# First group's values projected alone, VectorE exponentials from the first unit on, and the last output tile split over three engines

## The chip, the cores and the metric

The kernel runs on one core of a Trainium2 chip. The metric is the device time of one execution in microseconds (us). The engines are TensorE (PE, matrix products into PSUM), VectorE (DVE), ScalarE (ACT), GpSimd (POOL) and SyncE (SP, which issues most of the DMAs). A weight load of TensorE is shown as PEld.

## The reference

x is a 2048 x 512 bf16 matrix. Two branches are computed from it and mixed row by row with a gate:

```python
def _A_ref(x, wqkv, wo):            # 32 heads of 16
    qkv = (x @ wqkv).reshape(B, S, 3, H, Dh).transpose(2, 0, 3, 1, 4)
    q, k, v = qkv[0], qkv[1], qkv[2]
    scores = jnp.einsum("bhqd,bhkd->bhqk", q, k) * (Dh ** -0.5)
    p = softmax(scores, axis=-1)
    o = jnp.einsum("bhqk,bhkd->bhqd", p, v)
    return o.transpose(0, 2, 1, 3).reshape(B, S, D) @ wo

def _B_ref(x, w_gate, w_up, w_down):  # hidden size 1792
    return (silu(x @ w_gate) * (x @ w_up)) @ w_down

g = sigmoid((x * gate_w).sum(-1, keepdims=True))
out = g * _A_ref(x) + (1 - g) * _B_ref(x)
```

The attention has 32 x 2048 x 2048 exponentials. In the kernel they are 2048 banks of 128 keys x 512 queries.

## The kernel before

Heads are handled in eight groups of four, queries in four blocks of 512, keys in 16 tiles of 128. A unit is one group of heads for one block of queries; there are 32 units, in the order of `UNIT` (L114): group 0 for all four query blocks first, then the other groups block by block. Within a unit a slot is one key tile, with four banks, one for each head, so there are 512 slots and 64 banks to a unit. Group 0's keys and queries have a path of their own at the start: they are projected with zero-padded weights and need no DMA to reach the rows where the scores want them.

A bank is a product of keys and queries (`score`, L608) into PSUM. Then one of two engines takes the exponential. ScalarE takes banks in pairs (`emit_pair`, L621): one activation of 128x1024, tile s_t to tile e_t. VectorE takes them in blocks of four, one bank of each head of the group (`emit_d`, L641): for each bank one step from d_t to y_t, and for the four together six steps of 128x2048 on y_t, z_t and u_t, the last of which writes y_t. Afterwards `pv` (L720) multiplies by the values (vaug: for every head a column of ones and 16 columns of values; 32 columns are read, so those of the next head stand in the product too, in rows that nobody uses). A block whose unit has been closed by then gets its product in a bank of its own (x_ps) and an addition on VectorE.

The order of the instructions on TensorE, ScalarE and VectorE is written out at build time by a planner. It keeps a planned clock for each of the three engines (`Plan`), with a cost for each step, and emits what fits. Work that is not attention comes in chains of pieces (`Chain`, `Pacer`, L17 to L73), each with a slot of release and a due slot: projections of keys, queries and values, the gate, the two FFN products, the down product and the output product. `side` (L1069) gives out a piece only if the pacer has credit, which grows by slot with the most pressing due work. `begin` (L1059) forces chains that a slot needs. `force` emits all of a chain, and pays the VectorE steps owed to it. VectorE's steps are owed at emission and paid by `fill_dve` (L695): first the step of a waiting d_t, then owed evictions, then block steps. `to_vector` (L1086) says whether the next bank goes to VectorE: none in unit 0, no new block behind bank 50 of a unit (behind bank 4 in the last), none while three blocks are live or more than 6 us of block steps wait.

At the start SP issues the four transposing loads of x (L174), then the values' weights wv (512 columns, into the tile rb, L184) and the rest of wqk; ScalarE's queue issues the first 64 columns of the query and key weights (L178). GpSimd and VectorE set constants; lo_t, far_t and bsel (L245 to L248) are three small VectorE steps whose result the key bounds of later groups use (`k_bound`, L376). TensorE then projects group 0's keys and the first queries; VectorE reduces the keys' largest absolute values (kpart), makes kneg from them, TensorE multiplies that with the queries' absolute values (bp), and VectorE adds the bound to the queries (qx). In between stands `v_now` (L873), which projects four value tiles over all 512 columns, evicted by ScalarE. The other 12 value tiles are chains (`v_pieces`, L381) with due slot tt + 3, evicted by VectorE into vaug.

FFN chains are due between `f0` = 44 and `f1` = 504 (L944). They use the tile mt for the hidden activations.

After the last unit closes there is a tail: the output product for the last two groups in two parts (`last_mm`, L1168), reciprocals of the softmax sums, their product with the last unit's output (on_l), and `store` (L818) for each of the four output tiles: one VectorE step from PSUM, gate and an accumulated part (acc, which lies in kaug's memory), and one DMA issued by SP. All VectorE steps there follow each other in the written order.

Of the kernel before, what the change touches and what calls it, by code (L numbers as in the profile page):

```python
# [78 lines left out]
def kernel(  # L79
# [100 lines left out]

    rb = big.tile([P, NB, QBW], BF16, name="rb")
    wv = rb[:, :, :]

    nc.sync.dma_start(out=wv, in_=A_wqkv[:, 2 * D:3 * D].rearrange("(dc p) c -> p dc c", p=P))  # L184
    for c0 in (D, 0):
        nc.sync.dma_start(out=wqk[:, :, c0 + 64:c0 + D],
                          in_=A_wqkv[:, c0 + 64:c0 + D].rearrange("(dc p) c -> p dc c", p=P))
# [39 lines left out]
    for g in range(1, G):  # L227

        nc.vector.memset(kaug[:, g, :].bitcast(F32), 1.0019378662109375)
    vaug = big.tile([P, KT, G * 4 * VC + 16], BF16, name="vaug")  # L230
    nc.gpsimd.memset(vaug[:, :, G * 4 * VC:], 0.0)
    nc.gpsimd.memset(
        vaug[:, :, 0:G * 4 * VC].rearrange("p t (h c) -> p t h c", c=VC)[:, :, :, 0:1], 1.0)

# [5 lines left out]
    for h in range(8):  # L240
        c = 2 * (h % 4) + h // 4
        nc.gpsimd.memset(lo_t[:, c:c + 1], float(DH * h))
    far_t = const.tile([P, 8], F32, name="far_t")

    nc.vector.tensor_scalar(out=lo_t[:], in0=lo_t[:], scalar1=pidx[:, 0:1], scalar2=None, op0=ALU.subtract)  # L245
    nc.vector.tensor_scalar(out=far_t[:], in0=lo_t[:], scalar1=-float(DH) + 0.5, scalar2=-1.0,
                            op0=ALU.is_gt, op1=ALU.mult)
    nc.vector.scalar_tensor_tensor(out=bsel[:, :], in0=lo_t[:], scalar=0.5, in1=far_t[:],  # L248
                                   op0=ALU.is_lt, op1=ALU.mult)
# [131 lines left out]
    def v_pieces(tt, act_evac=False):  # L381
        st = {}

        def pc(h):
            def f():
                if h == 0:
                    st["p"] = m_tile("vp")
                for dc in (2 * h, 2 * h + 1):
                    mm(st["p"][:, 0:D], lhsT=xT[:, dc, tt * P:(tt + 1) * P], rhs=wv[:, dc, :],
                       start=(dc == 0), stop=(dc == DC - 1))  # L390
                spend("F", 2)
                if h == 1 and act_evac:
                    end()
                elif h == 1:
                    later(0.75, end)
            return f

        def end():
            dst = vaug[:, tt, 0:G * 4 * VC].rearrange("p (h c) -> p h c", c=VC)[:, :, 1:1 + DH]
            sv = st["p"][:, 0:D].rearrange("p (h c) -> p h c", c=DH)  # L400
            if act_evac:
                act(out=dst, in_=sv, func=ACT.Copy)
            else:
                vec.tensor_copy(out=dst, in_=sv)
            m_free(plan.pe if act_evac else plan.dve)
        return [(2, pc(0), True), (2, pc(1), False)]


# [311 lines left out]
    def pv(bs, last):  # L720


        un = bs[0] // (4 * KT)
        extra = un < closed
        if extra:
            o = m_tile("x_ps")
        else:
            if un not in o_of:
                while un and un - 1 not in osbs:
                    pay()  # L730
                plan.pe = max(plan.pe, o_end[0])
                o_of[un] = ps_o.tile([P, QBW], F32, tag="o", name="o_ps")
            o = o_of[un]
        for b in bs:
            n, j = b // 4, HEADS[b % 4]
            first = extra or (un, j) not in begun
            begun.add((un, j))
            c0 = (4 * UNIT[un][1] + j) * VC
            if n < KT and n in v_chain:
                force(v_chain[n])  # L740
            mm(o[32 * j:32 * j + 32, :], lhsT=vaug[:, n % KT, c0:c0 + 32], rhs=e_of.pop(b),
               start=first, stop=extra or last, tile_position=(0, 32 * j), skip_group_check=True)
            e_left.pop(b, None)
        spend("C", 1, max(e_end.pop(b, 0.0) for b in bs))
        if extra:
            def add():
                blocks[un] -= 1
                vec.tensor_tensor(out=(of_of if blocks[un] else osbs)[un][:, :], in0=of_of[un][:, :], in1=o[:, :],
                                  op=ALU.add)
                m_free(plan.dve)  # L750
                if not blocks[un]:
                    finish(un)
            later(0.6, add)
# [119 lines left out]
    def v_now(tt):  # L873
        for _, f, _ in v_pieces(tt, act_evac=True):
            f()

    act(out=q0r[:, :], in_=qp0[:, :], func=ACT.Copy)
    for i in range(2):
        vec.tensor_reduce(out=kpart0[:, i:i + 1], in_=kp0[i][:, :], axis=AX.X, op=ALU.max,
                          apply_absolute_value=True)  # L880
        vec.tensor_copy(out=ones_h[i][:], in_=onescol[:])
        v_now(i)
        act(out=kaug[:, 0, i * 2 * QBW:(i + 1) * 2 * QBW], in_=kp0[i][:, :], func=ACT.Identity,
            bias=ones_h[i][:, 0:1], scale=1.0)
        if i == 0:
            vec.tensor_scalar(out=kneg1, in0=bsel0, scalar1=kpart0[:, 0:1], scalar2=None, op0=ALU.mult)
            vec.tensor_scalar(out=aq0[:, :].bitcast(U16), in0=q0r[:, :].bitcast(U16), scalar1=0x7FFF, scalar2=None,
                              op0=ALU.bitwise_and)
    vec.scalar_tensor_tensor(out=kneg0, in0=bsel0, scalar=kpart0[:, 1:2], in1=kneg1,
                             op0=ALU.mult, op1=ALU.min)  # L890
    v_now(2)
# [7 lines left out]
    V0 = 4  # L899
    v_now(3)  # L900
    plan.dve = plan.act = plan.pe


    pace = Pacer()
    need = {}
    v_chain = {}
    for tt in range(V0, KT):
        v_chain[tt] = pace.add(v_pieces(tt), 0, tt + 3)
    prev = []
    for qb in range(1, QB):  # L910
        d = qb * KT
# [29 lines left out]
    order_ = [(qb, fc) for qb in range(QB) for fc in range(FC)]  # L941
    prev = []
    fin_prev = []
    f0, f1 = 44, SLOTS - 8  # L944
    per = (f1 - f0) / QB
    for qb in range(QB):
        a0 = f0 + per * qb
# [65 lines left out]
    def pv_ready(now):  # L1013

        if late and (now is None or late[0][0] <= now):
            un = late[0][1][0] // (4 * KT)
            if un == closed or un < closed and (now is None or m_ready() is not None and m_ready() <= now):
                return late[0][1]
        if done < SLOTS and done // KT == closed and not (now is not None and done in v_chain
                                                          and not v_chain[done].done()):  # L1020
            bs = [b for b in range(4 * done, 4 * done + 4) if b not in vset]
            if all(b in e_of for b in bs) and (now is None or max(e_end[b] for b in bs) <= now):
                if closed in o_of or now is None or (not closed or closed - 1 in osbs) and o_end[0] <= now:
                    return bs
        return None

    def pvs_ready(now):

        k = n = 0
        for ready, bs in late[:2]:  # L1030
            un = bs[0] // (4 * KT)
            if ready <= now and (un == closed or un < closed and k == 0 and m_ready() is not None and m_ready() <= now):
                k += 1
        for n in (done, done + 1):
            if n < SLOTS and n // KT == closed and not (n in v_chain and not v_chain[n].done()):
# [50 lines left out]
    def to_vector():  # L1086

        un, at_ = divmod(nxt, 4 * KT)
        if vcur:
            if nxt % 4 in [b % 4 for b in vcur["b"]]:  # L1090
                return 0
            return 2 if at_ >= 4 * KT - 4 * (NV - vcur["i"]) else 1
        if not un or at_ > (50 if un < UNITS - 1 else 4) or y_live[0] >= 3 or sum(v[0] for v in vops) > 6:
            return 0
        return 1

    while nxt < nb:
# [4 lines left out]
        if pairs[0] - min(e_left.values(), default=pairs[0]) >= EB - 1:  # L1102

            for m in (done, done + 1):
                while m in v_chain and not v_chain[m].out():
                    emit_piece(v_chain[m])
            next_pv()
            continue
        room = s_end[pairs[0] % 2] - plan.pe
# [110 lines left out]
```

## Time and profile before

| | |
|---|---|
| Median of 4 runs | 875.71 us (874.95 to 876.65) |
| Profiled execution, time | 874.95 us |
| Profiled execution, span | 873.2 us |
| First exponential starts / last one ends | 19.85 / 863.8 us |
| ScalarE busy | 845.4 us (97%) |
| TensorE busy | 799.7 us (92%) |
| VectorE busy | 786.9 us (90%) |
| GpSimd busy | 7.1 us |
| ScalarE exponentials (two banks each) | 882 |
| VectorE blocks (four banks each) | 71 |

A profile line of a group reads: line of the kernel (that of a helper, where one is used: L158 for matmuls, L161 for ScalarE, L167 for VectorE's ordered steps), engine, operation, output tile, input tiles, shapes and count; then busy time in all, mean ns of one; then the engine's idle time just before them, and what ended it. Instructions of an engine overlap a little, so starts are closer together than durations say. A matmul's duration includes its way through the array; consecutive ones start more closely than that.

### The profile page before, as it was taken

The page shows a single profiled execution, that of the slowest core. Times are in us where ns is not written, and L with a number is a line of the kernel's source. Part 1 is how long each engine was busy: PE and PEld are TensorE (multiplying, and loading weights), DVE is VectorE, ACT ScalarE, POOL GpSimd, SP SyncE. Part 2 cuts the span into 40 slices and gives each one's busy share as a digit, 9 for nine tenths or more (in the row PEclk, how much of TensorE's full clock was granted, in tenths as well). Part 3 has the DMA queues.
Part 4 walks back from the last instruction along what each step waited for, and adds up shares of the span by engine and source line. Part 5 has one row for each costly group of instructions (what it writes and reads, how often), then busy time and mean ns, then how long its engine had stood idle before and what let it go on. Part 6 is the DMA issues. An engine that isn't in the chain of part 4 may idle for free.

```text
span 873.2 us, 14286 instructions
## 1 busy us (share of the span) xinstructions
PE 799.7 (92%) x5168; PEld 207.8 (24%) x5168; DVE 786.9 (90%) x1103; ACT 845.4 (97%) x947; POOL 7.1 (1%) x29
## 2 busy tenths in 40 slices
PE   5999999999999899999989899899998989989986
PEld 2222222222222222222222222222222222222221
DVE  6379999999999999999999999999999998999984
ACT  3999999999999999999999999999999999999995
POOL 3000000000000000000000000000000000000000
PEclk9999999999999999999999999999999999999998
DMA  8301121131101112210011121110011121000000
GB/s 213 106 1 28 29 50 34 24 67 31 31 12 26 40 33 72 53 37 11 4 30 33 34 55 45 42 28 4 4 25 35 36 57 49 21 10 4 5 20 24
DMA packets 87535, 31.98 MB, mean 37 GB/s; under 512 B 75120, under 2 KB 87016, under 8 KB 87464
## 3 DMA queue, kind: packets, MB, share of 16 engines
q1 hardware_dynamic: 86408, 30.94, 14.4%
q8 instruction: 40, 0.66, 0.3%
q10 hardware_dynamic: 1056, 0.13, 0.1%
q14 instruction: 31, 0.25, 0.1%
HBM read 20.83 MB, written 2.34 MB: 27 GB/s over the span
## 4 chain that ended last, share of the span: by engine, by line
ACT 43%; PE 36%; issue 10%; DVE 9%; SPq 1%; DMA 1%; DVEq 0%; ACTq 0%
ACT e_t L161 39%; PE s_t L158 13%; PE o_ps L158 7%; DVE y_t L167 4%; PE d_t L158 4%; PE dps L158 4%; ACT th L161 3%; PE gp L158 3%; DVE u_t L167 2%; PE up L158 1%; PE qp L158 1%; SPq L174 1%; PE kp L158 1%; PE vp L158 1%; PE a_ps L158 1%
## 5 line engine op out<-in xcount | busy, mean ns | idle before, releaser
L161 ACT ACTIVATE e_t<-s_t 128x1024 bf16<-128x1024 f32 x882 | 821.9, 1079 | 4.4 <-PE s_t L158 3.1
L158 PE MATMUL s_t<-qx,kaug 64*128 64x512 bf16 x1656 | 330.2, 385 | 50.0 <-ACT e_t L161 48.1
L167 DVE TENSOR_SCALAR y_t<-d_t 128x512 uint16<-128x512 f32 x284 | 195.1, 687 | 29.7 <-PE d_t L158 26.3
L158 PEld LDWEIGHTS <-kaug 64*128 64x128 bf16 x2048 | 100.0, 93 | 379.0 <-issue 375.9
L158 PE MATMUL o_ps<-e_t,vaug 128*32 128x512 bf16 x1764 | 173.5, 388 | 0.4 <-ACT e_t L161 0.3
L158 PE MATMUL d_t<-qx,kaug 64*128 64x512 bf16 x264 | 99.6, 377 | 0.3 <-DVE y_t L167 0.3
L167 DVE TENSOR_TENSOR y_t<-y_t,u_t 128x2048 uint16<-128x2048 uint16 x71 | 86.6, 1219 | 0.9
L167 DVE TENSOR_TENSOR u_t<-u_t 128x2048 f16<-128x2048 f16 x71 | 86.5, 1218 | 0.8
L167 DVE TENSOR_TENSOR u_t<-u_t,z_t 128x2048 f16<-128x2048 f16 x71 | 86.4, 1217 | 0.4
L158 PEld LDWEIGHTS <-vaug 128*32 128x32 bf16 x2048 | 45.5, 94 | 133.3 <-issue 129.4
L158 PE MATMUL dps<-wd_t,mt 128*128 128x512 bf16 x224 | 67.8, 384 | 0.0
L158 PE MATMUL gp<-xT,wg 128*128 128x512 bf16 x224 | 67.8, 384 | 0.0
L158 PE MATMUL up<-xT,wu 128*128 128x512 bf16 x224 | 65.7, 384 | 0.0
L167 DVE TENSOR_SCALAR y_t<-y_t 128x2048 uint16<-128x2048 uint16 x71 | 48.9, 688 | 1.2
L167 DVE TENSOR_SCALAR u_t<-z_t 128x2048 f16<-128x2048 uint16 x71 | 48.7, 686 | 0.7
L167 DVE TENSOR_SCALAR z_t<-y_t 128x2048 uint16<-128x2048 uint16 x71 | 48.6, 684 | 0.1
L167 DVE SCALAR_TENSOR_TENSOR gs<-th,gp 128x512 bf16<-128x512 bf16 x56 | 38.2, 681 | 4.2 <-ACT th L161 3.7
L167 DVE SCALAR_TENSOR_TENSOR mt<-gs,up 128x512 bf16<-128x512 bf16 x56 | 38.2, 682 | 2.2
L161 ACT ACTIVATE th<-gp 128x512 bf16<-128x512 f32 x56 | 36.4, 650 | 0.0
L158 PEld LDWEIGHTS <-mt 128*128 128x128 bf16 x263 | 16.1, 99 | 42.9 <-issue 36.1
L158 PE MATMUL s_t<-on,kaug 64*128 64x512 bf16 x108 | 21.7, 383 | 3.1 <-ACT e_t L161 2.7
L158 PEld LDWEIGHTS <-wu 128*128 128x128 bf16 x224 | 13.7, 97 | 32.0 <-issue 27.6
(101 smaller groups left out, 352.8 us busy)
## 6 DMA issues: line engine op xcount, KB each, us to landing
wg<-in_B_w_gate_dram SPq DMA_DIRECT2D x56, 128.0 KB
wu<-in_B_w_up_dram SPq DMA_DIRECT2D x56, 128.0 KB
on<-osb SPq DMA_DIRECT2D x120, 16.0 KB
rb<-rr SPq DMA_DIRECT2D x15, 128.0 KB
wd_t<-in_B_w_down_dram SPq DMA_DIRECT2D x1, 1792.0 KB
qx<-qst SPq DMA_DIRECT2D x112, 16.0 KB
out_dram<-o_t SPq DMA_DIRECT2D x12, 128.0 KB
kaug<-on SPq DMA_DIRECT2D x20, 64.0 KB
```

Source lines behind the costliest of these rows:

```text
L158: ordered(nc.tensor.matmul(*args, **kw))
L161: ordered(nc.scalar.activation(*args, **kw))
L167: return lambda *a, **kw: ordered(f(*a, **kw))
L174: nc.sync.dma_start_transpose(out=xT[:, dc, :], in_=x[:, dc * P:(dc + 1) * P])
```

## The change

It has six parts.

1. Values' weights come in two loads: the first 64 columns (group 0) on ScalarE's queue, behind the first query and key weights; the other 448 on SP as before.
2. Group 0's values are projected alone, four key tiles into one bank (`v0_pieces`): the first four tiles before the first unit, in one place between the two reductions, evicted by one ScalarE step; the other three chains with due slots 5, 9 and 13. The other groups' values (`v_pieces`, now 448 columns) are 16 chains released at slot 2, due at slots 12 + 3 tt, and forced by the first product that needs them (unit 4, slot 64). `v_of` and `v_done` tell which chain a slot needs.
3. The steps for lo_t, far_t and bsel move behind the first queries' update, and kneg1 behind both reductions. GpSimd sets 16 more columns of vaug to zero.
4. `to_vector` allows VectorE's banks from bank 8 of unit 0 on, and in the last unit new blocks up to bank 24 (before: 4).
5. FFN chains start being due at slot 72 instead of 44, and `side` gives out a piece without credit if a chain needed within 12 slots is not out.
6. In the tail, tile 0 of the last output is scaled by ScalarE from PSUM into an f32 tile and added by GpSimd; VectorE stores tiles 1 to 3; tile 0's DMA is issued by SP behind theirs.

```diff
     wv = rb[:, :, :]
-    nc.sync.dma_start(out=wv, in_=A_wqkv[:, 2 * D:3 * D].rearrange("(dc p) c -> p dc c", p=P))
+    nc.scalar.dma_start(out=wv[:, :, 0:64], in_=A_wqkv[:, 2 * D:2 * D + 64].rearrange("(dc p) c -> p dc c", p=P))
+    nc.sync.dma_start(out=wv[:, :, 64:D], in_=A_wqkv[:, 2 * D + 64:3 * D].rearrange("(dc p) c -> p dc c", p=P))
...
+    nc.gpsimd.memset(vaug[:, :, 4 * VC:4 * VC + 16], 0.0)
...
-    nc.vector.tensor_scalar(out=lo_t[:], in0=lo_t[:], scalar1=pidx[:, 0:1], scalar2=None, op0=ALU.subtract)
...
+    def v0_pieces(t0, act_evac=False):
+        st = {}
+        def pc(i):
+            def f():
+                if i == 0:
+                    st["p"] = m_tile("vp")
+                for dc in range(DC):
+                    mm(st["p"][:, 64 * i:64 * i + 64], lhsT=xT[:, dc, (t0 + i) * P:(t0 + i + 1) * P],
+                       rhs=wv[:, dc, 0:64], start=(dc == 0), stop=(dc == DC - 1))
+                spend("F", V0_MM)
+                if i == 3 and act_evac:
+                    end()
+                elif i == 3:
+                    later(0.35, end)
+            return f
+        def end():
+            dst = vaug[:, t0:t0 + 4, 0:4 * VC].rearrange("p t (h c) -> p t h c", c=VC)[:, :, :, 1:1 + DH]
+            sv = st["p"][:, 0:256].rearrange("p (t h c) -> p t h c", h=4, c=DH)
+            if act_evac:
+                act(out=dst, in_=sv, func=ACT.Copy)
+            else:
+                vec.tensor_copy(out=dst, in_=sv)
+            m_free(plan.pe if act_evac else plan.dve)
+        return [(V0_MM, pc(i), i == 0) for i in range(4)]
+    V0_MM = 1.8
+    def v_pieces(tt):
...
-                    mm(st["p"][:, 0:D], lhsT=xT[:, dc, tt * P:(tt + 1) * P], rhs=wv[:, dc, :],
+                    mm(st["p"][:, 64:D], lhsT=xT[:, dc, tt * P:(tt + 1) * P], rhs=wv[:, dc, 64:D],
                        start=(dc == 0), stop=(dc == DC - 1))
...
-        v_now(i)
         act(out=kaug[:, 0, i * 2 * QBW:(i + 1) * 2 * QBW], in_=kp0[i][:, :], func=ACT.Identity,
             bias=ones_h[i][:, 0:1], scale=1.0)
         if i == 0:
-            vec.tensor_scalar(out=kneg1, in0=bsel0, scalar1=kpart0[:, 0:1], scalar2=None, op0=ALU.mult)
             vec.tensor_scalar(out=aq0[:, :].bitcast(U16), in0=q0r[:, :].bitcast(U16), scalar1=0x7FFF, scalar2=None,
                               op0=ALU.bitwise_and)
+        if i == 0:
+            for _, f, _ in v0_pieces(0, act_evac=True):
+                f()
+    vec.tensor_scalar(out=kneg1, in0=bsel0, scalar1=kpart0[:, 0:1], scalar2=None, op0=ALU.mult)
...
-    for tt in range(V0, KT):
-        v_chain[tt] = pace.add(v_pieces(tt), 0, tt + 3)
+    for i in range(1, KT // 4):
+        v_chain[i] = pace.add(v0_pieces(4 * i), 0, 4 * i + 1)
+    v_rest = [pace.add(v_pieces(tt), 2, int(12 + 3 * tt)) for tt in range(KT)]
+    def v_of(n):
+        if n < KT:
+            return v_chain.get(n // 4)
+        return v_rest[n - QB * KT] if QB * KT <= n < QB * KT + KT else None
...
-    f0, f1 = 44, SLOTS - 8
+    f0, f1 = 72, SLOTS - 8
...
-        c = pace.next(plan.slot) if pace.credit > 0 else None
+        due = any(not c.out() for n in range(plan.slot, plan.slot + 12) for c in need.get(n, []))
+        c = pace.next(plan.slot) if pace.credit > 0 or due else None
...
-        if not un or at_ > (50 if un < UNITS - 1 else 4) or y_live[0] >= 3 or sum(v[0] for v in vops) > 6:
+        if nxt < 8 or at_ > (50 if un < UNITS - 1 else 24) or y_live[0] >= 3 or sum(v[0] for v in vops) > 6:
             return 0
...
-    for tq in range(TQ):
-        store(qb * TQ + tq, a_ps[tq], acc[0][:, tq, :], mt[:, tq, :])
+    t0 = qb * TQ
+    scaled = work.tile([P, QBW], F32, tag="of", name="scaled", bufs=1)
+    act(out=scaled[:, :], in_=a_ps[0][:, 0:D], func=ACT.Identity, scale=gval[:, t0:t0 + 1])
+    nc.gpsimd.tensor_tensor(out=mt[:, 0, :], in0=scaled[:, :], in1=acc[0][:, 0, :], op=ALU.add)
+    for tq in range(1, TQ):
+        store(t0 + tq, a_ps[tq], acc[0][:, tq, :], mt[:, tq, :])
+    nc.sync.dma_start(out=out_f[t0 * P:(t0 + 1) * P, :], in_=mt[:, 0, :])
```

More of the change, by code (lines that the diff above doesn't have):

```diff
@@ L243 @@
     far_t = const.tile([P, 8], F32, name="far_t")
-    nc.vector.tensor_scalar(out=lo_t[:], in0=lo_t[:], scalar1=pidx[:, 0:1], scalar2=None, op0=ALU.subtract)
[L246 to L249, printed above, removed]
     nc.gpsimd.memset(wo_l[:], 0.0)
@@ L379, in k_bound @@
                           scalar2=None, op0=ALU.mult)
-    def v_pieces(tt, act_evac=False):
+    def v0_pieces(t0, act_evac=False):
[24 more added lines that the diff above has]
+    def v_pieces(tt):
         st = {}
@@ L388, in f @@
                 for dc in (2 * h, 2 * h + 1):
-                    mm(st["p"][:, 0:D], lhsT=xT[:, dc, tt * P:(tt + 1) * P], rhs=wv[:, dc, :],
+                    mm(st["p"][:, 64:D], lhsT=xT[:, dc, tt * P:(tt + 1) * P], rhs=wv[:, dc, 64:D],
                        start=(dc == 0), stop=(dc == DC - 1))
                 spend("F", 2)
[L392 to L395, printed above, removed]
+                if h == 1:
+                    later(0.7, end)
             return f
         def end():
[L399 to L405, printed above, removed]
+            dst = vaug[:, tt, 4 * VC:G * 4 * VC].rearrange("p (h c) -> p h c", c=VC)[:, :, 1:1 + DH]
+            vec.tensor_copy(out=dst, in_=st["p"][:, 64:D].rearrange("p (h c) -> p h c", c=DH))
+            m_free(plan.dve)
         return [(2, pc(0), True), (2, pc(1), False)]
@@ L738, in pv @@
             c0 = (4 * UNIT[un][1] + j) * VC
-            if n < KT and n in v_chain:
-                force(v_chain[n])
+            if v_of(n) is not None:
+                force(v_of(n))
             mm(o[32 * j:32 * j + 32, :], lhsT=vaug[:, n % KT, c0:c0 + 32], rhs=e_of.pop(b),
@@ L872 @@
     kneg1 = mt[:, 3, 2 * P:3 * P]
-    def v_now(tt):
-        for _, f, _ in v_pieces(tt, act_evac=True):
-            f()
     act(out=q0r[:, :], in_=qp0[:, :], func=ACT.Copy)
@@ L885 @@
         if i == 0:
-            vec.tensor_scalar(out=kneg1, in0=bsel0, scalar1=kpart0[:, 0:1], scalar2=None, op0=ALU.mult)
             vec.tensor_scalar(out=aq0[:, :].bitcast(U16), in0=q0r[:, :].bitcast(U16), scalar1=0x7FFF, scalar2=None,
                               op0=ALU.bitwise_and)
+        if i == 0:
+            for _, f, _ in v0_pieces(0, act_evac=True):
+                f()
+    vec.tensor_scalar(out=kneg1, in0=bsel0, scalar1=kpart0[:, 0:1], scalar2=None, op0=ALU.mult)
     vec.scalar_tensor_tensor(out=kneg0, in0=bsel0, scalar=kpart0[:, 1:2], in1=kneg1,
                              op0=ALU.mult, op1=ALU.min)
-    v_now(2)
     bp0 = ps_d.tile([P, QBW], F32, tag="d", name="bp0")
@@ L898 @@
                                  in1=q0[0][:, v, :], op0=ALU.mult, op1=ALU.add)
-    V0 = 4
-    v_now(3)
+    vec.tensor_scalar(out=lo_t[:], in0=lo_t[:], scalar1=pidx[:, 0:1], scalar2=None, op0=ALU.subtract)
+    vec.tensor_scalar(out=far_t[:], in0=lo_t[:], scalar1=-float(DH) + 0.5, scalar2=-1.0,
+                            op0=ALU.is_gt, op1=ALU.mult)
+    vec.scalar_tensor_tensor(out=bsel[:, :], in0=lo_t[:], scalar=0.5, in1=far_t[:],
+                                   op0=ALU.is_lt, op1=ALU.mult)
     plan.dve = plan.act = plan.pe
@@ L906, with v_done @@
     v_chain = {}
-    for tt in range(V0, KT):
-        v_chain[tt] = pace.add(v_pieces(tt), 0, tt + 3)
+    for i in range(1, KT // 4):
[5 more added lines that the diff above has]
+        return v_rest[n - QB * KT] if QB * KT <= n < QB * KT + KT else None
+    def v_done(n):
+        return v_of(n) is None or v_of(n).done()
     prev = []
@@ L1018, in pv_ready @@
                 return late[0][1]
-        if done < SLOTS and done // KT == closed and not (now is not None and done in v_chain
-                                                          and not v_chain[done].done()):
+        if done < SLOTS and done // KT == closed and (now is None or v_done(done)):
             bs = [b for b in range(4 * done, 4 * done + 4) if b not in vset]
@@ L1034, in pvs_ready @@
         for n in (done, done + 1):
-            if n < SLOTS and n // KT == closed and not (n in v_chain and not v_chain[n].done()):
+            if n < SLOTS and n // KT == closed and v_done(n):
                 bs = [b for b in range(4 * n, 4 * n + 4) if b not in vset]
@@ L1104 @@
             for m in (done, done + 1):
-                while m in v_chain and not v_chain[m].out():
-                    emit_piece(v_chain[m])
+                while v_of(m) is not None and not v_of(m).out():
+                    emit_piece(v_of(m))
             next_pv()
```

## The prediction

> **What bounds the kernel now.** I read the page's head first, then the groups of instructions, then the chain that ended last, then busy times by stretch, and last the order of time at both ends.
>
> ```profile
> PE 799.7 (92%) x5168; PEld 207.8 (24%) x5168; DVE 786.9 (90%) x1103; ACT 845.4 (97%) x947; POOL 7.1 (1%) x29
> ...
> L161 ACT ACTIVATE e_t<-s_t 128x1024 bf16<-128x1024 f32 x882 | 821.9, 1079 | 4.4 <-PE s_t L158 3.1
> L158 PE MATMUL s_t<-qx,kaug 64*128 64x512 bf16 x1656 | 330.2, 385 | 50.0 <-ACT e_t L161 48.1
> L167 DVE TENSOR_SCALAR y_t<-d_t 128x512 uint16<-128x512 f32 x284 | 195.1, 687 | 29.7 <-PE d_t L158 26.3
> ```
>
> The reader is to see ScalarE as the bound of the body: 882 exponentials with only 4.4 us of idle before them all, while TensorE waits 48.1 us for ScalarE. TensorE and VectorE are close behind. The first exponential starts at 19.85 us and the last ends at 863.8, so the span of 873.2 is 19.85 of start, 844 of ScalarE, 9.4 of tail. In a stretch of 27 exponentials (25.04 us with one whole 1.08 at the end) the pitch is (25.04-1.08)/26 = 0.922 us for a pair of banks. A block of four banks that VectorE takes is two pairs: 1.84 us less of ScalarE.
>
> The start and its chain:
>
> ```profile
> 10.10 4.73 DMA rb<-in_A_wqkv_dram
> 14.87 1.04 PE vp L158 x4
> 15.93 0.60 ACT vaug L161
> 16.53 1.00 ACT kaug L161
> 17.53 0.49 ACT vaug L161
> 18.02 1.01 ACT kaug L161
> 19.02 0.97 ACT vaug L161 x2
> ```
>
> Columns: start, duration, what. The first exponential stands behind the whole values load (rb, 4.73 us) and four ScalarE evictions of values. Of the DMA queues in the first 20 us, the one that ScalarE issued to (packets, MB, share of the time of 16 engines):
>
> ```profile
> q10 hardware_dynamic: 1056, 0.13, 4.2%
> ```
>
> ```profile
> 20.00:48.00 28.00, 26.77 (x164) 7.08 (x162) 10.16 (x15) 28.00 (x31) 0.00 (x0) 1.00 0.35 95
> 48.00:76.00 28.00, 27.22 (x172) 6.74 (x170) 24.64 (x37) 27.37 (x31) 0.00 (x0) 1.00 0.01 4
> 836.00:864.00 28.00, 23.01 (x152) 6.09 (x149) 18.29 (x29) 27.27 (x30) 0.00 (x0) 0.90 0.01 3
> ```
>
> Columns: stretch, length, busy PE, PEld, DVE, ACT, POOL, then clock, DMA share, GB/s. VectorE works 10 of 28 us in the first unit and 18 in the last one, against 26 to 27 in the body. TensorE is full in the first unit.
>
> **The change part by part.** The sum is made against the profiled execution (span 873.2, time 874.95; the median of the runs is 875.71, 0.76 more).
>
> *Start.* Now TensorE begins the values at 14.87, when rb lands, and the bound's product bp, queued behind 12 of them, starts at 17.46 though its operand is ready at 16.28 and TensorE is free from 13.58. After: 16 products of 64 columns need only the small load. Each lies between the 4-column dt products (0.24/4 = 0.06) and the vp ones (0.215); I take 0.1, so they end at about 15.2 and bp waits only for VectorE. On VectorE far_t and bsel (0.16 each) leave the place between the two reductions and kneg1 (0.25) moves behind the second, so kneg0 still ends near 16.2. bp then starts at 16.35 instead of 17.46: 1.1 us earlier, and so do the two qx updates (1.41) and the first scores. ScalarE keeps pace: q0r to 14.2, kaug to 15.4, one smaller value eviction to 15.9, kaug to 17.0. Its bound is the 19.99 at which its last value eviction ends now.
> The small load is a third transfer on ScalarE's queue, ahead of the table load; ScalarE is idle until 13.61, so its 0.5 us of issue is free. Its packets are like those of the two wqk loads: 4.2% of 20 us is 0.84 us of all 16 engines for two, so 0.42 for one, and the engines are full (share 1.0 and more from 4 to 12 us) with the transposes that gate the last kp products at 12.34. Net -0.7; ends -1.1 (the load hides in a gap) and +0.4 (bp gains nothing). The page "DMA: Bandwidth & Descriptors" of the Trainium skill, Specifications, asks for at least 512 B per transfer and so speaks against a slice of 128 B rows; by it the load is worse than its bytes, which the row of that queue already holds.
> The moved bsel steps have their first user many slots on; the added zeroing on GpSimd is like the one of 0.31 us there, and GpSimd ends at 8.0 us with the first value eviction near 15: both nothing, at worst 0.4 of VectorE if it were already loaded.
>
> *VectorE's banks in unit 0.* From 23 us to 48 VectorE is idle about 15.7 us, and 3.4 in the next 28, where the body leaves about 1.5: 15.7 - 1.3 (5% stays idle) + 1.9 = 16.3. Against it stand the evictions: now 12 of 0.69 in the body = 8.3; after, 16 of 448 columns at 0.6 (between 0.41 and 0.69) and 3 of 256 at 0.4, 10.8 to 11.1, so 2.8 more. Left 13.5 us. A block costs VectorE (by the rows of y_t, z_t and u_t) 4 x 0.687 + 0.684 + 0.686 + 0.688 + 1.218 + 1.217 + 1.219 = 8.46, and by 32 late additions of 0.68 for 71 blocks 0.3 more: 8.8. That is 1.5 blocks, 1.5 x 1.84 = -2.8 us. The ends are 0 (the blocks come here and are missing later) and three blocks, -5.5.
>
> *TensorE.* Does it have room? At measured pitches unit 0 costs now: 32 score pairs at 0.33, 16 value products at 0.30, 24 projection pieces at 0.53, three q0 pieces at 0.53: 29.7 for 29.5 us of ScalarE, full. After, for 28 pairs (25.8 us): 9.2 + 8 single banks at 0.21 = 1.7, 4.8, twelve first-group pieces at 0.5 (four weight loads of 0.096 and a switch of 0.1) = 6.0, q0 1.6: 23.3, and 2.5 left for five of 32 rest pieces at 0.48. The other 27, 13 us, go to slots 16 to 60, out of which the FFN start (slot 44 to 72) takes 28 slots of about 0.37 us = 10.3. That work returns between slots 72 and 504, where the 48 us that TensorE waits for ScalarE can cover it. I take +0.5; ends 0 and +3.0 (a third of the 10.3 shows). The queue behind each rest eviction is VectorE's: products of the first group read 15 columns of the next group's values, so a late rest eviction holds TensorE; the evictions come in emission order with spare slots, hence nothing, inside the same upper end.
>
> *Last unit.* A second block may start up to bank 24. VectorE is free of the unit-30 work at 845.7 and then has the three on products 1.1, block one 5.4 by starts, four a_ps steps 2.6; the second block adds 4 x 0.62 + 5.4. Together 17.0, to 862.7 without a gap, 863.7 with one us of the 3.9 that it now waits for a_ps. ScalarE ends 1.84 earlier, at 862.0, against 863.8. So only about half a us is left: -0.5; ends -1.8 and +2.7 (all gaps stay: 866.6).
>
> *Tail.*
>
> ```profile
> 867.75 1.41 DVE L167 SCALAR_TENSOR_TENSOR mt<-al,gval,kaug 128x512 bf16<-128x512 f32 x2
> 868.53 2.31 SPq L823 DMA_DIRECT2D out_dram<-mt  x4
> 869.08 1.40 DVE L167 SCALAR_TENSOR_TENSOR mt<-a_l,gval,kaug 128x512 bf16<-128x512 f32 x2
> ```
>
> Four VectorE steps at 0.68 end at 870.48; the last of four stores (0.35 to issue) goes out at 870.5. After, three end at about 869.9, and store four waits for ScalarE (0.6, from 867.6) and GpSimd's add. That add has no row: between half of the 0.951 of a 128x1024 fill and the 2.27 of the strided 128x512 one; nearest is the select, which reads and writes, 0.292 for 128, so 1.17 for 512. It ends at about 869.5; the last store, behind tile 3's on SP, goes at 870.2. -0.3; ends -0.5 and +0.3. The Trainium skill, "GPSIMD Engine Reference", Performance versus the Vector engine, gives GpSimd twice VectorE's time for such an add and keeps elementwise work on VectorE; by its 4.5 us for 2048 columns the add would be 1.1 us, still hidden by three VectorE steps, an estimate that no row here shows.
>
> Sum: -0.7 - 2.8 + 0.5 - 0.5 - 0.3 = -3.8: 871.2 for the profiled execution, 872.0 for the median.
>
> **The rivals.**
> *More blocks (chance 0.18).* Three blocks in unit 0 kept to the end, and the last one's block in full: -0.7 - 5.5 - 1.8 - 0.3 = -8.3, 867.4. For it: 17 idle us. Against it: VectorE is at 26 to 27 of 28 after that, so the evictions moved later displace blocks.
> *The gain is eaten by TensorE (0.22).* One block net, and the denser TensorE makes ScalarE wait 2.5: -0.7 - 1.8 + 2.5 = 0.0, 874 to 876.5. For it: 27.22 of 28 busy in the second stretch, with the idle of 0.43 us before an exponential at 56.56. Against it: TensorE's 48 us of waiting. The same time results if the change doesn't do what it says, blocks in unit 0 being taken from later ones: -0.7, 875.
> *Slower (0.10).* A third block in the last unit. It is started if the second has its four banks by bank 24 with no more than 6 us of VectorE steps planned ahead. Then 7.9 us more stand before the end, 863.7 becomes 871.6, +7.8 on that path, with the rest -3.3 net: +4 to +5, 880. It decides from about 5 us of lateness on. Against it: VectorE is busy with reciprocals until 845.7, so those six us are still planned when the second is full.
> The forecast itself has 0.50: 869.5 to 873.9.
>
> **How the numbers follow.** A measurement here tells about 0.2% (1.75 us): 873.96 to 877.46 is the same. Faster takes the forecast 0.50 and the first rival 0.18, and a little of the second: 0.70. Same: most of the second, 0.19. Slower: the third and an end of the unknowns, 0.11. The range leaves a tenth on each side: 867.3 to 876.6. The forecast's own is 869.5 to 873.9.
>
> **What would show it.** Start: first exponential near 19.1 with no value load in the chain. Blocks: y_t steps from about 23 us, 72 to 74 final y_t steps instead of 71, fewer exponentials at the same 0.92 pitch. TensorE: idle before exponentials under 8 us in all. Last unit: final y_t step near 863. Tail: 9 us from the last exponential. Wrong would be: no fall in exponentials, or ScalarE waiting for scores in the first 100 us, or a last y_t step after 865.

## The result and the profile after

The changed kernel takes 877.45 us at the median, the kernel before 875.81 us in the runs beside it. The ratio is 1.0019, with a 95% interval from 1.0012 to 1.0026: 0.19% slower, where 0.42% faster was forecast, and outside the forecast range (867.3 to 876.6). The profiled execution has a span of 875.5 us against 873.2.

The head of the page and the groups of exponentials and of VectorE's bank steps, after:

```profile
PE 805.2 (92%) x5232; PEld 210.2 (24%) x5232; DVE 806.8 (92%) x1133; ACT 840.3 (96%) x941; POOL 8.7 (1%) x31
...
L161 ACT ACTIVATE e_t<-s_t 128x1024 bf16<-128x1024 f32 x878 | 818.1, 1092 | 5.0 <-PE s_t L158 3.8
...
L167 DVE TENSOR_SCALAR y_t<-d_t 128x512 uint16<-128x512 f32 x292 | 200.6, 687 | 33.3 <-PE d_t L158 30.1
```

VectorE has 73 blocks (292 banks) instead of 71, ScalarE four exponentials less. So VectorE did take banks off ScalarE, as forecast. The span splits as follows:

| | before | after | difference |
|---|---|---|---|
| first exponential starts | 19.85 | 20.14 | +0.3 |
| from there to the end of the last one | 843.95 | 838.97 | -5.0 |
| from there to the end of the span | 9.4 | 16.4 | +7.0 |

The body won 5.0 us, and the end lost 7.0. The end of the changed kernel in order of time (start, duration, engine, line, operation, tiles; in brackets the idle time before it, and what ended it):

```profile
863.60 0.69 DVE L167 TENSOR_SCALAR y_t<-y_t 128x2048 uint16<-128x2048 uint16 x1
864.21 0.68 DVE L167 COPY of<-o_ps 128x512 f32<-128x512 f32 x1
864.35 0.62 PE L158 MATMUL x_ps<-y_t,vaug 128*32 128x512 bf16 x4 [4.78 <-DVE y_t L167]
...
868.24 1.03 PE L158 MATMUL al<-wo_l,on_l 128*128 128x512 bf16 x2 [0.40 <-DVE on_l L167]
869.06 1.06 PE L158 MATMUL a_l<-wo_l,on_l 128*128 128x512 bf16 x2
869.31 0.69 ACT L161 ACTIVATE scaled<-al,gval 128x512 f32<-128x512 f32 x1 [10.20 <-PE al L158]
870.03 0.75 DVE L167 SCALAR_TENSOR_TENSOR mt<-al,gval,kaug 128x512 bf16<-128x512 f32 x1 [1.25 <-ACT scaled L161]
870.08 1.27 POOL L1225 TENSOR_TENSOR mt<-scaled,kaug 128x512 bf16<-128x512 f32 x1 [861.73 <-ACT scaled L161]
870.70 1.40 DVE L167 SCALAR_TENSOR_TENSOR mt<-a_l,gval,kaug 128x512 bf16<-128x512 f32 x2
871.37 0.37 SPq L1228 DMA_DIRECT2D out_dram<-mt  x1
871.84 1.38 SPq L845 DMA_DIRECT2D out_dram<-mt  x3
```

Three things are to be seen. The last exponential ended at 859.11, but TensorE stands 4.78 us until the last step of the last unit's second block. Behind that its products run at half speed: the last two into al, of 512 columns each, take 1.03 us where they took 0.60 before:

```profile
867.11 0.60 PE L158 MATMUL al<-wo_l,on_l 128*128 128x512 bf16 x2 [0.40 <-DVE on_l L167]
```

And in the stores VectorE waits for ScalarE's scaling, and SP issues tile 0's store (L1228) first, not last: the other three stand behind it until GpSimd is done at 871.35.

Three stretches of the start, of before and then of after (columns: stretch, length, busy PE, PEld, DVE, ACT, POOL with instructions, then granted clock, DMA share, GB/s):

```profile
15.00:20.00 5.00, 4.77 (x23) 1.86 (x22) 3.22 (x7) 4.07 (x7) 0.00 (x0) 1.00 0.69 217
20.00:30.00 10.00, 9.22 (x58) 2.41 (x55) 2.77 (x4) 10.00 (x12) 0.00 (x0) 1.00 0.98 265
30.00:40.00 10.00, 9.91 (x60) 2.59 (x57) 5.32 (x8) 10.00 (x12) 0.00 (x0) 1.00 0.00 1
```

```profile
15.00:20.00 5.00, 1.86 (x21) 0.91 (x19) 4.59 (x11) 2.99 (x4) 0.00 (x0) 0.85 0.89 287
20.00:30.00 10.00, 9.86 (x66) 3.12 (x65) 3.36 (x9) 8.80 (x10) 0.00 (x0) 0.56 0.93 258
30.00:40.00 10.00, 9.65 (x68) 2.73 (x68) 9.90 (x16) 10.00 (x13) 0.00 (x0) 1.00 0.05 9
```

After the change TensorE works 1.86 of the five us before the first exponential, where it worked 4.77, and in the ten us behind that its granted clock is 0.56 instead of 1.00. ScalarE, the bound, then works 8.80 of 10 us instead of 10. What TensorE does around bp, the bound's product, before and then after:

```profile
14.87 2.75 PE L158 MATMUL vp<-rb,xT 128*128 128x512 bf16 x12 [1.29 <-DMA rb<-in_A_wqkv_dram]
17.46 0.38 PE L158 MATMUL bp<-aq,mt 128*128 128x512 bf16 x1
```

```profile
15.34 0.63 PE L158 MATMUL vp<-rb,xT 128*128 128x64 bf16 x16
18.26 0.39 PE L158 MATMUL bp<-aq,mt 128*128 128x512 bf16 x1 [2.29 <-DVE mt L167]
19.49 1.36 PE L158 MATMUL s_t<-qx,kaug 64*128 64x512 bf16 x4 [0.84 <-DVE qx L167]
```

The 16 small value products are done in 0.63 us, and TensorE then stands 2.29 us ahead of bp and 0.84 us behind it.

### The profile page after: what moved, and what is told of

Its sections match the earlier page's. It is cut to its first block, busy times and chain, and to the rows that moved or that the text cites. A ratio compares the mean times of both kernels' runs of the same rounds, so it can differ in the third digit from the quotient of the medians.

```text
span 875.5 us, 14437 instructions
## 1 busy us (share of the span) xinstructions
PE 805.2 (92%) x5232; PEld 210.2 (24%) x5232; DVE 806.8 (92%) x1133; ACT 840.3 (96%) x941; POOL 8.7 (1%) x31
## 4 chain that ended last, share of the span: by engine, by line
PE 45%; ACT 37%; issue 8%; DVE 7%; DMA 1%; SPq 1%; DVEq 0%; ACTq 0%
ACT e_t L161 34%; PE s_t L158 16%; PE o_ps L158 8%; PE d_t L158 5%; PE dps L158 4%; PE gp L158 3%; DVE y_t L167 3%; ACT th L161 3%; DVE u_t L167 2%; PE up L158 2%; PE qp L158 1%; PE vp L158 1%; PE kp L158 1%; PE a_ps L158 1%; PE x_ps L158 1%
## 5 line engine op out<-in xcount | busy, mean ns | idle before, releaser
L167 DVE TENSOR_SCALAR y_t<-d_t 128x512 uint16<-128x512 f32 x292 | 200.6, 687 | 33.3 <-PE d_t L158 30.1
L158 PE MATMUL o_ps<-e_t,vaug 128*32 128x512 bf16 x1756 | 170.5, 387 | 0.0
L158 PE MATMUL d_t<-qx,kaug 64*128 64x512 bf16 x276 | 104.9, 380 | 0.3 <-DVE y_t L167 0.3
L167 DVE TENSOR_TENSOR u_t<-u_t 128x2048 f16<-128x2048 f16 x73 | 89.0, 1219 | 0.9
L167 DVE TENSOR_TENSOR y_t<-y_t,u_t 128x2048 uint16<-128x2048 uint16 x73 | 89.0, 1219 | 0.7
L167 DVE TENSOR_TENSOR u_t<-u_t,z_t 128x2048 f16<-128x2048 f16 x73 | 88.8, 1217 | 0.4
L158 PE MATMUL vp<-rb,xT 128*128 128x448 bf16 (+1 forms) x128 | 22.2, 286 | 0.0
```

Source lines behind the costliest of these rows:

```text
L158: ordered(nc.tensor.matmul(*args, **kw))
L167: return lambda *a, **kw: ordered(f(*a, **kw))
```

## The experiments

All ratios are to the kernel before in runs beside it; the changed kernel itself has 1.0019 [1.0012, 1.0026].

| kernel | median us | ratio | 95% interval |
|---|---|---|---|
| last unit's limit back at 4 (e1_last4) | 873.31 | 0.9967 | 0.9948 to 0.9985 |
| no split of the last tile (e2_nosplit) | 875.64 | 1.0003 | 0.9986 to 1.0020 |
| kernel before with limit 24 (e3_before24) | 877.79 | 1.0021 | 1.0006 to 1.0037 |
| idle products at the start (e4_warm) | 875.43 | 0.9987 | 0.9975 to 0.9999 |
| e1, e2 and e4 together (e5_combined) | 869.64 | 0.9918 | 0.9892 to 0.9943 |
| e1 and a PSUM tile of its own (e6_owntile) | 872.40 | 0.9956 | 0.9938 to 0.9975 |
| e1 without banks in unit 0 (e7_nounit0) | 877.85 | 1.0016 | 1.0001 to 1.0031 |
| e1 and the small load on SP (e8_loadsp) | 871.75 | 0.9943 | 0.9921 to 0.9964 |
| e4, e6 and the store on ScalarE's queue (e9_actqueue) | 869.71 | 0.9937 | 0.9920 to 0.9955 |
| idle products in the last wait (e10_tailwarm) | 876.67 | 1.0004 | 0.9988 to 1.0020 |
| kernel before with e4's products (e11_beforewarm) | 878.62 | 1.0031 | 1.0018 to 1.0043 |

### The last unit's second block

```diff
-        if nxt < 8 or at_ > (50 if un < UNITS - 1 else 24) or y_live[0] >= 3 or sum(v[0] for v in vops) > 6:
+        if nxt < 8 or at_ > (50 if un < UNITS - 1 else 4) or y_live[0] >= 3 or sum(v[0] for v in vops) > 6:
```

> The changed kernel with the last unit's limit for a new VectorE block back at bank 4. Theory A (the second block of the last unit ends after ScalarE, TensorE waits for it 4.8 us and falls to half clock for the tail): two more exponentials (880), from the last exponential to the end about 9.5 to 10.5 us instead of 16.4, time 870 to 873. Theory B (the tail is long because of the split of the last output tile): the tail stays at 14 us or more, time 877 to 879.

Measured: 873.31 us, ratio 0.9967, against 1.0019 for the changed kernel: 0.52%, 4.6 us. 880 exponentials, the last one ends at 860.89, and the span ends 9.5 us later. Its end in order of time:

```profile
860.95 0.39 PE L158 MATMUL o_ps<-e_t,vaug 128*32 128x512 bf16 x2 [0.52 <-ACT e_t L161]
861.27 0.60 PE L158 MATMUL al<-wo_l,osb 128*128 128x512 bf16 x2
861.38 0.69 DVE L167 CAST osb<-o_ps 128x512 bf16<-128x512 f32 x1 [1.68 <-PE o_ps L158]
```

TensorE follows ScalarE again, and VectorE waits for TensorE (1.68 us), not the other way round. Theory A holds, with a time just above its 870 to 873; the split, still in this kernel, is not what made the tail long. The reverse test puts the limit alone into the kernel before:

```diff
-        if not un or at_ > (50 if un < UNITS - 1 else 4) or y_live[0] >= 3 or sum(v[0] for v in vops) > 6:
+        if not un or at_ > (50 if un < UNITS - 1 else 24) or y_live[0] >= 3 or sum(v[0] for v in vops) > 6:
```

> The kernel before with only the last unit's limit raised from bank 4 to bank 24. Theory A: 880 exponentials instead of 882, but the tail behind the last one grows by 5 us or more: 878 to 881. Theory B: two exponentials less and an unchanged tail: 874.

Measured: 877.79 us, ratio 1.0021: slower by 1.8 us, though two exponentials fewer are done. The last exponential ends at 861.54, and the block later:

```profile
863.54 0.69 DVE L167 TENSOR_SCALAR y_t<-y_t 128x2048 uint16<-128x2048 uint16 x1
864.15 0.68 DVE L167 COPY of<-o_ps 128x512 f32<-128x512 f32 x1
864.28 0.62 PE L158 MATMUL x_ps<-y_t,vaug 128*32 128x512 bf16 x4 [2.30 <-DVE y_t L167]
```

The sign is A's, though the tail grew by 3.8 us only (13.2 against 9.4), not by 5. What matters is where VectorE ends: at 864.2 here and at 864.3 in the changed kernel, which had ScalarE ready 2.4 us earlier. VectorE, idle for only 0.8 of the last 20 us before that here and for 1.3 in the changed kernel, sets the end, and what ScalarE wins by giving banks to VectorE only lengthens TensorE's wait, from 2.30 to 4.78.

### Half clock behind that wait

```diff
+        if extra and un == UNITS - 1:
+            warm_ps = ps_d.tile([P, QBW], F32, tag="d", name="warm_ps")
+            for _ in range(18):
+                mm(warm_ps[:, :], lhsT=xT[:, 0, 0:P], rhs=xT[:, 0, 0:QBW], start=True, stop=True)
```

> The changed kernel with 18 products on x, whose result nobody reads, while TensorE waits for the last block of the last unit. If the half clock after that wait is part of the loss: TensorE at full clock behind the wait, the stretch from the last block step to the end 9.7 to 10.3 us instead of 11.3, time 1 to 1.5 us below the changed kernel, 876 to 876.5. If only the wait itself counts: 877.4.

The clock behind the wait, after and in this kernel, in the same columns as above:

```profile
864.00:876.00 12.00, 5.03 (x32) 1.75 (x31) 4.79 (x11) 0.69 (x1) 1.27 (x1) 0.50 0.13 44
```

```profile
865.00:875.00 10.00, 3.05 (x32) 1.27 (x31) 4.53 (x11) 0.69 (x1) 1.27 (x1) 0.90 0.15 52
```

The clock is 0.90 instead of 0.50, and 1.00 as long as TensorE works (its last product ends at 869.1, the clock falls at 873.01). From the start of x_ps to the end of the span it takes 9.9 us instead of 11.2. So the half clock costs 1.3 us of the tail by the traces; by the times the gain is 0.15% (1.3 us), with intervals that overlap. The wait itself stays.

### The start

```diff
+    nc.vector.memset(kaug[:, 1, :].bitcast(F32), 1.0019378662109375)
+    warm_ps = ps_o.tile([P, QBW], F32, tag="o", name="warm_ps")
+    def warm(n):
+        for _ in range(n):
+            mm(warm_ps[:, :], lhsT=kaug[:, 1, 0:P], rhs=kaug[:, 1, 0:QBW], start=True, stop=True)
...
+    warm(9)
     kp0 = [ps_s.tile([P, 2 * QBW], F32, tag="s", name="kp0") for _ in range(2)]
...
+    warm(8)
     bp0 = ps_d.tile([P, QBW], F32, tag="d", name="bp0")
     mm(bp0[:, :], lhsT=kneg0, rhs=aq0[:, :], start=True, stop=True)
+    warm(3)
```

> The changed kernel with products on constants, whose result nobody reads, in TensorE's idle places of the start (9 before the keys' projection, 8 before the bound's product, 3 behind it); a constant's zero filling order on VectorE moves with it. Theory C (at the start the change lost the work that held TensorE's clock up): full clock from about 9 us on without a fall until the tail, first exponential at 18.9 or before instead of 20.1, no idle of ScalarE in the ten us after it, 875 to 876. Theory D (the start is late because the third small load delays the transposes, and the clock does not matter): first exponential still at 19.8 or later, 877 to 878.

Measured: 875.43 us, ratio 0.9987; its interval lies wholly under that of the changed kernel, 0.32% or 2.8 us apart. ScalarE after its first exponential, in the changed kernel and then here (start, duration, what, count, idle before):

```profile
20.14 4.93 ACT L161 ACTIVATE e_t<-s_t 128x1024 bf16<-128x1024 f32 x5 [1.34 <-PE s_t L158]
25.33 1.02 ACT L161 ACTIVATE e_t<-s_t 128x1024 bf16<-128x1024 f32 x1 [0.26 <-PE s_t L158]
26.86 1.94 ACT L161 ACTIVATE e_t<-s_t 128x1024 bf16<-128x1024 f32 x2 [0.50 <-PE s_t L158]
28.98 109.76 ACT L161 ACTIVATE e_t<-s_t 128x1024 bf16<-128x1024 f32 x119 [0.19 <-PE s_t L158]
```

```profile
19.59 117.10 ACT L161 ACTIVATE e_t<-s_t 128x1024 bf16<-128x1024 f32 x127 [1.15 <-PE s_t L158]
```

The stretch from 20 to 30 us of this kernel, in the columns of the stretches above:

```profile
20.00:30.00 10.00, 8.53 (x79) 3.37 (x80) 5.41 (x11) 10.00 (x12) 0.00 (x0) 1.00 0.88 255
```

The granted clock is 1.00, and ScalarE no longer stops. In the seven profiles with the new start and without these products it stopped for 0.3 to 2.9 us in its first 15 us, and for longer where the clock was half for longer: 0.28 us with 3.4 us of half clock (e7), 0.76 with 6.8 (e6), 0.95 and 0.98 with 10.2 (the changed kernel, e1), 2.88 with 13.7 (e2, e8, e10). That part of theory C holds. The other part does not: the first exponential came at 19.59 only, since the transposes landed late here and the clock was half from 13.23 to 16.64 us. First exponentials of the new start lie between 18.3 and 20.1 from one profile to the next, those of the old one at 19.85 and 20.2.

This gain reaches the end. The last exponential ends at 857.05 and VectorE's last block step at 862.23, both 2.1 us earlier than in the changed kernel, and TensorE's wait between them is the same:

```profile
862.28 0.62 PE L158 MATMUL x_ps<-y_t,vaug 128*32 128x512 bf16 x4 [4.77 <-DVE y_t L167]
```

The control:

> The kernel before with the same idle products at the start as in the run that added them to the changed kernel. If they help only because the change emptied TensorE there: no change, within 0.1% of the kernel before, or slower by up to 1 us, since TensorE is busy with values there. If they help any start: 1 us or more faster.

Its edit is the same, put into the kernel before. Measured: 878.62 us, ratio 1.0031, 2.7 us slower, more than the us that was allowed for. bp starts at 19.73 us instead of 17.46, since eight products more stand ahead of it behind the values, and the first exponential comes at 22.16 instead of 19.85. So these products are no remedy by themselves: they help where the change had emptied TensorE.

The small load was moved as well:

```diff
-    nc.scalar.dma_start(out=wv[:, :, 0:64], in_=A_wqkv[:, 2 * D:2 * D + 64].rearrange("(dc p) c -> p dc c", p=P))
+    nc.sync.dma_start(out=wv[:, :, 0:64], in_=A_wqkv[:, 2 * D:2 * D + 64].rearrange("(dc p) c -> p dc c", p=P))
```

> The changed kernel with the last unit's limit back at 4 and the small load of values' weights issued by SP behind the four transposes instead of by ScalarE ahead of them. If that load delays the transposes: the second transpose's issue takes 2.8 us instead of 3.4 to 3.6, the keys' last products start 0.4 to 1 us earlier, time 872.3 to 873. If the clock and not the load sets the start: 873.3, and the first exponential stays between 18.3 and 20.1.

Measured: 871.75 us, ratio 0.9943 against 0.9967 for e1, with overlapping intervals. The second transpose's issue took 3.75 us, so it was not shortened; with the load ahead it took 3.2 to 3.6. In the three profiles of the old start, which has no such load, it took 2.84 (the kernel before), 3.00 (e11) and 3.62 us (e3). So the issue is as long without the load ahead, and these traces give no sign that the load delays the transposes; what does, no run tells.

### The split of the last tile

```diff
-    scaled = work.tile([P, QBW], F32, tag="of", name="scaled", bufs=1)
-    act(out=scaled[:, :], in_=a_ps[0][:, 0:D], func=ACT.Identity, scale=gval[:, t0:t0 + 1])
-    nc.gpsimd.tensor_tensor(out=mt[:, 0, :], in0=scaled[:, :], in1=acc[0][:, 0, :], op=ALU.add)
-    for tq in range(1, TQ):
+    for tq in range(TQ):
...
-    nc.sync.dma_start(out=out_f[t0 * P:(t0 + 1) * P, :], in_=mt[:, 0, :])
```

> The changed kernel with the last four output tiles all stored by VectorE, as before. Theory A: the wait of 4.8 us for the last block stays, only VectorE's wait for ScalarE's scaling (0.7 us) goes, against one more VectorE step of 0.7: time within 0.7 us of the changed kernel, 876.7 to 878. Theory B: 5 us or more are gained, 872.5 or less.

Measured: 875.64 us, ratio 1.0003; the intervals of this and the changed kernel overlap. The wait for the last block stays (4.77 us), so B falls again. The traces tell more: from the first store step of tile 0 (ScalarE's scaling or VectorE's step) to the end of the span it takes 6.24 us with the split, 5.41 without, and 5.47 in the kernel before. By the traces the split costs 0.8 us; the times are too close to tell. Why, e6 and e9 ask:

```diff
-    a_ps = [al[:, 0:QBW], al[:, QBW:2 * QBW]]
-    a_ps += [ps_m.tile([P, QBW], F32, tag="m", name="a_l")[:, :] for _ in range(2)]
+    a_l = [ps_m.tile([P, QBW], F32, tag="m", name="a_l")[:, :] for _ in range(2)]
+    a_ps = [a_l[0], al[:, 0:QBW], al[:, QBW:2 * QBW], a_l[1]]
```

> The changed kernel with the last unit's limit back at 4, and with the tile that ScalarE scales in a PSUM tile of its own instead of one that it shares with the next output tile. Theory E (VectorE waits for ScalarE's scaling because both read one PSUM tile): VectorE's first store step starts without waiting for ScalarE, the end comes 0.5 to 0.8 us earlier than with the limit alone (872.6). Theory F (the wait comes from the split itself): the wait of about 0.7 us stays, 873.3.

Measured: 872.40 us, ratio 0.9956 against 0.9967, not told apart. In the trace the wait is gone as theory E says, and the stretch to the end is still 6.22 us:

```profile
863.35 0.69 ACT L161 ACTIVATE scaled<-a_l,gval 128x512 f32<-128x512 f32 x1 [3.08 <-PE a_l L158]
863.78 1.41 DVE L167 SCALAR_TENSOR_TENSOR mt<-al,gval,kaug 128x512 bf16<-128x512 f32 x2 [0.32 <-PE al L158]
864.12 1.26 POOL L1225 TENSOR_TENSOR mt<-scaled,kaug 128x512 bf16<-128x512 f32 x1 [855.73 <-ACT scaled L161]
865.40 0.36 SPq L1228 DMA_DIRECT2D out_dram<-mt  x1
865.86 1.38 SPq L845 DMA_DIRECT2D out_dram<-mt  x3
```

VectorE's first store step ended at 864.5, but SP held it until tile 0's store had gone out at 865.40, when GpSimd was done. So the wait of VectorE did not set the end; SP's order did, as the next kernel bears out. There tile 0's store goes to ScalarE's queue, with e4's products in the kernel too:

```diff
-    nc.sync.dma_start(out=out_f[t0 * P:(t0 + 1) * P, :], in_=mt[:, 0, :])
+    nc.scalar.dma_start(out=out_f[t0 * P:(t0 + 1) * P, :], in_=mt[:, 0, :])
```

> The changed kernel with the last unit's limit back at 4, the idle products at the start, the scaled tile in a PSUM tile of its own, and that tile's store issued on ScalarE's queue. If SP's queue (tile 0's store stands ahead of the other three there and waits for GpSimd) is what the split loses by once VectorE no longer waits: the last store goes out 0.5 to 1 us earlier after the last product than with the own tile alone, and the time is 869 to 869.6, at or just under the combination without the split (869.6). If the split costs in another way: 870 or more.

```profile
862.02 0.69 ACT L161 ACTIVATE scaled<-a_l,gval 128x512 f32<-128x512 f32 x1 [3.08 <-PE a_l L158]
863.23 1.65 SPq L851 DMA_DIRECT2D out_dram<-mt  x3
864.09 0.37 ACTq L1237 DMA_DIRECT2D out_dram<-mt  x1
```

Measured: 5.23 us from the scaling to the end of the span, one us less than in e6, and 0.2 less than without the split. The time, 869.71 us with ratio 0.9937, is not told apart from e5's; no run changes the queue alone.

### Unit 0's banks, and all together

```diff
-        if nxt < 8 or at_ > (50 if un < UNITS - 1 else 4) or y_live[0] >= 3 or sum(v[0] for v in vops) > 6:
+        if not un or at_ > (50 if un < UNITS - 1 else 4) or y_live[0] >= 3 or sum(v[0] for v in vops) > 6:
```

> The changed kernel with the last unit's limit back at 4 and no VectorE banks in unit 0. If the blocks of unit 0 are what shortened the body: 70 or 71 blocks, 882 to 884 exponentials, 1.8 to 3.7 us slower than with the limit alone, 875 to 877. If the projection in two parts shortened it by itself: 873.3, unchanged.

Measured: 877.85 us, ratio 1.0016 against e1's 0.9967: 4.3 us slower, more than the upper expectation. It has 70 blocks and 884 exponentials, e1 has 72 and 880:

```profile
L161 ACT ACTIVATE e_t<-s_t 128x1024 bf16<-128x1024 f32 x884 | 823.8, 1090 | 6.1 <-PE s_t L158 5.3
```

Unit 0's banks are two blocks. Without them the changed kernel has one block less than the kernel before (70 against 71), so the net is one. Which part takes that one, the longer evictions, the later FFN start or the pieces given out without credit, no run tells apart.

> The changed kernel with the last unit's limit back at 4, all four last tiles stored by VectorE, and the idle products at the start. If the three effects add (about -4 us by the first, -1.5 by the second, -2 by the third, from 877.4): 869 to 871, ratio to the kernel before 0.993 to 0.995. If they overlap: 872 or more.

Measured (the edit is those of e1, e2 and e4): 869.64 us, ratio 0.9918, interval 0.9892 to 0.9943. That is what adding the effects gives: 1.0019 less 0.0052, 0.0016 and 0.0032 is 0.9919, though the middle one alone is not clear of noise. This is the best version measured, with e9 beside it, 0.8% faster than the kernel before.

## Why the prediction was wrong

*Unit 0's blocks* held. Forecast 1.5 blocks net, -2.8 us; there were two taken and one given back elsewhere, one net, -1.84 us by the 0.92 us that a pair costs (e1, e7).

*TensorE's room* held for the body: ScalarE is idle for 5.0 us before its exponentials against 4.4, but 1.34 of the 5.0 stand before the first one and 0.95 in the ten us of half clock behind it. So the projections that moved into the body, priced at +0.5, do not show as waiting, and the rival in which a denser TensorE eats the gain found no support.

*The last unit* is the step that failed most: -0.5 was forecast, -1.8 to +2.7 allowed, and by e1 it is +4.6. The two ends were well placed for the kernel before: VectorE was to end at 862.7 to 863.7 and did at 864.2 in e3, ScalarE at 862.0 and did at 861.5. The first error is in the sum. The last unit ends with the later of two paths, and after the second block that is VectorE's. The -2.8 us for the blocks of unit 0 were still subtracted in full, though they shorten ScalarE's path alone: from e3 to the changed kernel, whose first exponentials start alike (20.18 and 20.14), ScalarE's end came 2.4 us earlier and VectorE's did not move (864.2, 864.3). What is won at the start does reach both ends (e4). In the changed kernel ScalarE ended at 859.1 and waited in vain. The second error is what follows the block: 11.3 us from its last step to the end of the span, where the sum had 9.1 behind the last exponential; 1.3 of them are the half clock (e10) and 0.8 the split (e2). One row shown in the prediction pointed there and went unused: the last unit's granted clock of 0.90. The slower rival named the right place but asked for a third block; the second was enough.

*The start*: -0.7 was forecast, with the first exponential near 19.1; the changed kernel's profile has 20.14, the other profiles of its start without added products 18.3 to 19.0. That step was about right in the mean of these seven, 18.8. It is no fixed gain, though: counted from the start of the last of the keys' products, the first exponential came 5.0 to 5.5 us later with the new start, and 6.9 (the kernel before) and 5.4 (e3) with the old one. Missing was a price for the cover that it removed. The 12 value products that bp waited behind also kept TensorE busy; without them TensorE stands 2.29 and 0.84 us, and ScalarE then pays up to 2.9 us, for scores at half clock. This cost stood in the sum as nothing. Keeping TensorE busy gave 2.8 us (e4).

*The tail*: -0.3 was forecast, and it is +0.8 by the traces. The add on GpSimd took 1.27 us where 1.17 was taken, but the step "the last store, behind tile 3's on SP" was wrong: SP's order is the built program's, not the text's, and tile 0's store stood first (e6, e9).

The trace's sum is +0.3 at the start, -5.0 in the body, +7.0 at the end, +2.3; the times say +1.6. The body's 5.0 is 3.7 for four exponentials; 0.7 is less idle time behind the first one (3.7 against 4.4), and what the other 0.6 are, no run here tells.

## What to carry to other kernels

Where two engines run beside each other to the end, work moved between them is priced at the end by the later path, and gains on the other path alone are not subtracted from it: find which engine's last step comes last, and whether it has gaps left. Before work is taken off an idle-looking stretch, ask what it kept going; here the removed products held TensorE's clock up. Where a store waits for a slow engine, give it a queue of its own (one us by the trace here), and read the order of a queue from the trace, not from the text.

## What the runs showed of the hardware

TensorE's granted clock fell to half after short gaps, not only after long ones. In the changed kernel it fell at 18.53 us: TensorE had worked 1.12 of the 3.41 us before, with a gap of 2.29 us in them; the gap of 0.84 us came behind the fall. The clock then was half until 28.77 us, through ten us in which TensorE was nearly always busy (9.86 of 10). At the start of e10 it was half for 13.7 us. In the kernel before it fell at 844.85 us, with no gap longer than 0.53 us in the 3.4 us before, in which TensorE worked 2.04 us:

```profile
843.84 0.39 PE L158 MATMUL s_t<-qx,kaug 64*128 64x512 bf16 x2 [0.52 <-ACT e_t L161]
844.76 0.57 PE L158 MATMUL s_t<-qx,kaug 64*128 64x512 bf16 x2 [0.53 <-ACT e_t L161]
```

The page "TensorE: Matmul & The Clock Gate" of the Trainium skill (HAM oscillation) asks for no gaps over some 3.4 us; here a gap of 2.29 us and gaps of 0.5 us stood before the fall, and the measurement decides.

The first exponential of one and the same start moved between 18.3 and 20.1 us from profile to profile, with the moment at which the last of the keys' products started (13.3 to 14.7 us). The landing of the transposes and the clock, which rose between 9.2 and 15.1 us in the seven profiles without added products, both bear on that moment; how much each, no run tells apart.
